# A written order for the second and third unit of an HGRN2 attention with a quick-GELU MLP, and w_in stored by pairs of blocks

## The chip, the cores and the metric

The kernel runs on one core of a Trainium2 chip. A core has TensorE (PE, matrix products; loads of its stationary operand are shown as PEld), VectorE (DVE), ScalarE (ACT), GpSimd (POOL) and SyncE (SP). SP, and here and there ACT, issue the transfers (SPq and ACTq in the profile), which the core's 16 DMA engines carry out. The metric is the device time of one execution in microseconds (us); less is better.

## The reference

Four batches, eight heads, 768 tokens and heads of 48 go through a gated linear recurrence; its output, laid out as 3072 tokens of 384, goes through an MLP with a hidden width of 2048.

```python
f = 1.0 / (1.0 + np.exp(-f_logit))
for t in range(S):
    state = f[:, :, t, :, None] * state + np.einsum('bhd,bhe->bhde', k[:, :, t], v[:, :, t])
    y[:, :, t] = np.einsum('bhd,bhde->bhe', q[:, :, t], state)
x = y.transpose(0, 2, 1, 3).reshape(B * S, H * D)
h = x @ w_in                                   # 384 -> 2048
g = h * (1.0 / (1.0 + np.exp(-1.702 * h)))
out = g @ w_out                                # 2048 -> 384
```

The weights come in as 64-bit floats; the kernel makes 32-bit floats of them itself.

## The kernel before

**Units.** The tokens go in 12 units of 256 (`U`), three to a batch. `attention(n)` makes the parts of unit n's attention, `mlp_unit` and `mlp_block` its MLP. In unit n the tokens are cut into chunks of 64. Within a chunk the recurrence goes through six levels (`level`, or `levels` two at a time from unit 2 on): PE makes scores (L442, into the tile `sc`), DVE multiplies the gates into q and k (`promote`, L536 or L540), ACT copies keys and queries aside for the next level (`set_aside`: Kc L511, Qc L517), and `evacuate` moves the scores into A (DVE L483 and L502, ACT L492). Then k is turned by PE (`turn_k`, L615, copied by ACT L616), PE adds the chunk's own products (`add`, L552) and makes the state products (L663), and DVE sums the states (L688, L689). The read-out (L710) takes the states; ACT copies it to yT (L725, `half(0)` and `half(1)`), and `to_x` sends it by transfers into xT, the MLP's operand. A half has three transfers: one of 144 KB (L777) and two of 32 and 16 KB (L782).

**Ahead of a unit's levels** its f, q and k are turned: from unit 2 on by DVE (`turn`, L361). f goes through the sigmoid on ACT (L391) and POOL (L388), and POOL makes the gates' products (`begin_gates`, L433). `load_raw` loads f (0), q (1) and k (2) of the next unit, `load_v` its v.

**Weights.** `pairs` lists 16 pairs of blocks of 128 hidden units in the order of use: for each of four rows r two pairs of w_in, then two of w_out. `fetch_weights` issues the transfer of the next pair's 64-bit words on SP's queue (768 KB; there are three buffers, `bits`, so pair m + 3 waits for the passes of pair m that read its buffer). `begin_pair` puts one ACT pass over the high words (L239) into ACT's queue at once and three DVE passes into `todo`: `low` (L235), `high` (L228, which needs ACT's pass) and `both` (L238, which writes the weights). A call of `convert` issues one of these passes, begins the next pair when few are left, and after a pair's last one calls `fetch_weights`.

**MLP of units 0 and 1.** Row by row: `mlp_h` has an item for each block (three products of 256 columns, L1125, then the gelu on ACT, L1129), `mlp_o` one for each block and half of the tokens (a product of 384 columns, L1139); ACT and DVE sum them (L1189, L1191). A row of a unit is 4 `h` items and 8 `o` items. These items are the list `fill`; each names how many blocks of weights (`state["done"]`) it needs. An `o` item needs its whole row. Unit 2 is like them at first, then uses sums of weights: `sums_of_w` makes sums of thirds of a row of blocks (`WA`, L954 and L952), and `sums_in_place` writes some of them over w_in itself, four on POOL and five on DVE. From unit 3 on the first layer is 20 products of such sums (`mlp_h20`, L1031), the second seven (`mlp_o7`, L893).

**Order.** `opening()` writes out unit 0's attention and unit 1's beginning. Then `follow(1, ...)`, `follow(2, ...)` and `follow(3, ...)` run the parts of a unit, which `parts_of` lists; behind each part `PLAN` says how many items of `fill`, conversions and chores (sums of weights) are issued. An item whose weights are not done in the program's order is left out there and comes later. To `follow(2)` the order of every engine is the one in which the program issues; later, that of PE and POOL alone. From unit 4 on `merge` spreads the items over the parts. `HOLES` puts conversions inside unit 2's levels. `keep_up` issues products that nobody reads (L116, 320 columns; each call takes one of four banks in turn), three ahead of unit 1's level 1 and three behind it.

The parts of unit 1 are: read-out of unit 0 and level 0; levels 1 to 5; two turns of k (T); states (S); its own read-out (W); turning f of unit 2 (B); turning q and loading v (B); gates and turning k with its first copies (B). Of unit 2: levels 0 and 1, 2 and 3, 4 and 5 (V); f and q of unit 3 (B); two T; k of unit 3 (B); S.

Of the kernel before, what the change touches and what calls it, by code (L numbers as in the profile page):

```python
# [23 lines left out]
def kernel(  # L24
# [33 lines left out]
    nc = tc.nc  # L58
# [108 lines left out]

    w_in = const.tile([P, NK, DFF], F32, name="w_in")
    w_out = const.tile([P, NFF, DM], F32, name="w_out")
# [25 lines left out]
    def fetch_weights(engine=nc.sync):  # L195
        n = state["fetch"]
        if n >= len(pairs) or n - PAIRS_AHEAD >= state["done"] // 2:
            return
        state["fetch"] += 1
        dst, parts = pairs[n]  # L200
        if moe_w_in.dtype == F32:
            for part, src in parts:
                nc.sync.dma_start(out=part(dst), in_=src)
            return
        bits = wp.tile([P, 2 * DM * 2], I32, tag="bits", name=f"bits_{n}", bufs=PAIRS_AHEAD)
        by_dst = bits.rearrange("p (c f) -> p c f", c=dst.shape[1])
        for part, src in parts:
            engine.dma_start(out=part(by_dst), in_=src.bitcast(I32))
        fetched[n] = by_dst.rearrange("p c (f two) -> p c f two", two=2)

    def begin_pair(m):
        if m not in fetched:
            todo.append(None)
            return
# [29 lines left out]
        todo.extend((high, both, None))  # L244

    def convert():

        if state["begin"] < len(pairs) and len(todo) <= NOP // 2:
            begin_pair(state["begin"])
            state["begin"] += 1  # L250
        if todo and todo[0]:
            todo.pop(0)()
        if todo and todo[0] is None:
            todo.pop(0)
            state["done"] += 2
            fetch_weights()


    HOLES = {(N_FILL, 0): 3, (N_FILL, 1): 2, (N_FILL, 2): 1, (N_FILL, 4): 1}

    def convert_in(n, l):

        for _ in range(HOLES.get((n, l), 0)):
            convert()

# [69 lines left out]
    def attention(n):  # L335
# [357 lines left out]
        def _():  # L693
# [26 lines left out]
            def half(h):  # L720
                for g in range(h, NG):
                    for f in (1, 0):
                        at, step = (g * HS, 1) if f else (U - 1 - g * HS, -1)
                        to, of = (rows(h), columns(h, g)) if g else (slice(0, HS + D),) * 2
                        nc.scalar.copy(view(yT[to], at, [[U, NP], [step, HS]]), py[of, g, :, f, :])  # L725
                two = (nc.scalar, nc.sync) if h and n < N_FILL else (nc.sync,)
                to_x(lambda h: (yT[rows(h), :NK], lambda r, d: yT[r:r + d, NK]), xT[:, :, :U], NG, (h,), two)
# [13 lines left out]
            xTs[n] = xT  # L741
            if n == 0:
                fetch_weights()
            if n > N_FILL:
# [181 lines left out]
    lanes = {}  # L926
    WA = {f"a{i}{c}": w_in[:, c, ROW[i] * FG * P:(ROW[i] + 1) * FG * P] for i in range(ROWS) for c in range(NK)}
    assert ROWS == 4 and NK == 3 and FG == 4

    def sums_of_w(names):  # L930

        for name in names:
            if name == "p16":
                WA[name] = wp.tile([P, 2 * DM], F32, tag="s", name="N_p16", bufs=1)[:, :FG * P]
            else:
                WA[name] = const.tile([P, FG * P], F32, name=f"N_{name}")
        first = (
            ("c3", "a30", "", "a32"), ("p15", "a21", "+", "a31"), ("c2", "a11", "+", "a12"), ("p6", "c2", "+", "a22"),
# [59 lines left out]
    def mlp_h20(n, g, before):  # L998
# [24 lines left out]
        def product(x, group, lane):  # L1023
# [5 lines left out]
            for t in range(wide):  # L1029
                f = group * wide + t  # L1030
                nc.tensor.matmul(  # L1031
                    ph[:, t], lhsT=WA[a][:, f * P:(f + 1) * P], rhs=E[n][b], start=(root and t == 0), stop=not goes_on,
                    skip_group_check=True,
# [77 lines left out]
    def mlp_h(n, ffs, g):  # L1111
        t = {}

        def one(ff, c):
            if c == 0:
# [9 lines left out]
            nc.tensor.matmul(  # L1125
                ph, lhsT=w_in[:, c, ff * P:(ff + 1) * P], rhs=xTs[n][:, c, :], start=(c == 0), stop=(c == NK - 1)
            )
# [4 lines left out]
    def mlp_o(n, ffs, g, done):  # L1132
# [3 lines left out]
        def one(tt, ff):  # L1136
# [68 lines left out]
    def parts_of(n):  # L1205
# [12 lines left out]
        if n + 1 < NALL:  # L1218
# [9 lines left out]
            else:  # L1228
# [23 lines left out]
    def merge(n, fill, columns, share):  # L1252
# [17 lines left out]
        state["behind"] = max(0, columns - done)  # L1270

    def follow(n, fill, plan):

        parts = parts_of(n)
        assert len(parts) == len(plan), (n, [kind for kind, _ in parts])
        done = 0
        for (kind, fn), (n_fill, n_ops, n_chores) in zip(parts, plan):
# [4 lines left out]
            done += 1  # L1282
            jobs = [convert] * n_ops + chores[:n_chores]
            del chores[:n_chores]
            if (n, done) == (1, 2):
                keep_up(3)
            for i in range(n_fill):
                for job in jobs[len(jobs) * i // n_fill:len(jobs) * (i + 1) // n_fill]:
                    job()
                if fill and fill[0][2] <= state["done"]:  # L1290
                    fill.pop(0)[1]()
            if not n_fill:
                for job in jobs:
                    job()

# [8 lines left out]
    def opening():  # L1304
# [44 lines left out]
        for _ in range(NOP):  # L1349
            convert()  # L1350

    fill = []
    opening()
    WAITS = {(1, "W", 1): 3}
    PLAN = {
# [4 lines left out]
    }  # L1360
# [4 lines left out]
    follow(2, fill, PLAN[2])  # L1365
    fill_order.close()
    while chores:
        chores.pop(0)()
# [47 lines left out]
```

## Time and profile before

| | |
|---|---|
| median of 3 runs | 594.89 us (593.5 to 596.12) |
| the profiled execution | 595.5 us, its span 593.2 us |
| PE busy | 568.8 us (96%) |
| weight loads on PE | 518.0 us (87%) |
| DVE busy | 438.1 us (74%) |
| ACT busy | 288.4 us (49%) |
| POOL busy | 139.2 us (23%) |
| moved by DMA | 60.34 MB, 102 GB/s in the mean |

The span is that of the instructions in one profiled execution; times in rows are microseconds from its start. In a timeline a row merges neighbouring instructions of one kind: start, duration, engine, line, operation, what is written from what, the number of records, and in brackets the idle time of the engine before and what ended it. In a table of stretches each row gives the length, then the busy time of PE, PEld, DVE, ACT and POOL with the number of instructions, the granted clock of PE (1.00 is full), the busy share of the DMA engines and GB/s. A 32-bit product appears as two records.

### The profile page before, as it was taken

The numbers are of one execution on the slowest core, as the hardware profiler recorded it, in microseconds if no ns is written. First come the engines' busy times: TensorE is split into PE (matmuls) and PEld (weight loads), VectorE is DVE, ScalarE is ACT, GpSimd is POOL, SyncE is SP. The second block draws the span as 40 slices with busy tenths as digits, with TensorE's granted clock in tenths as the row PEclk, the third lists the DMA queues.
The fourth block names the chain that finished last, engine by engine and source line by source line (L and its number), as shares of the span: only waits on it lengthen the run. The fifth ranks groups of instructions, "written<-read, shape, count | busy, mean of one in ns | idle before, by whom it ended". The sixth has DMA issues, their size and how long they took to land.

```text
span 593.2 us, 18507 instructions
## 1 busy us (share of the span) xinstructions
PE 568.8 (96%) x7832; PEld 518.0 (87%) x7832; DVE 438.1 (74%) x697; ACT 288.4 (49%) x588; POOL 139.2 (23%) x226
## 2 busy tenths in 40 slices
PE   7979888999999999999999999999999999999997
PEld 6756565867789999999999999999999999999997
DVE  2897767885989788798777798786987786461284
ACT  4754435424452474474474573573663563552440
POOL 3020020155235510600700700700701602203000
PEclk9989988999999999999999999999999999999999
DMA  7869958352363353453452343453352121001000
GB/s 185 189 183 221 232 138 223 75 129 61 104 150 75 104 124 82 98 127 90 121 140 57 86 114 94 118 143 63 92 146 59 46 55 29 28 3 27 28 1 28
DMA packets 86771, 60.34 MB, mean 102 GB/s; under 512 B 33505, under 2 KB 78465, under 8 KB 86689
## 3 DMA queue, kind: packets, MB, share of 16 engines
q1 hardware_dynamic: 86128, 58.40, 39.7%
q8 instruction: 62, 1.02, 0.7%
q10 hardware_dynamic: 561, 0.75, 0.5%
q14 instruction: 20, 0.16, 0.1%
HBM read 45.49 MB, written 8.91 MB: 92 GB/s over the span
## 4 chain that ended last, share of the span: by engine, by line
PE 83%; DVE 6%; ACT 5%; DMA 3%; issue 2%; ACTq 1%; SPq 0%; DVEq 0%
PE h L1031 16%; PE o_Y L893 13%; PE h L1125 10%; PE o_Z L893 9%; PE sc L442 6%; PE h_y L1031 6%; PE o L1139 6%; PE o_X L893 5%; PE o_W L893 4%; DMA bits<-in_moe_w_in_dram 2%; PE y L710 2%; PE y L552 2%; PE sc L663 2%; DVE X L540 1%; DVE g L1059 1%
## 5 line engine op out<-in xcount | busy, mean ns | idle before, releaser
L540 DVE TENSOR_TENSOR X<-X,tot 128x1024 f32<-128x1024 f32 x50 | 67.6, 1351 | 39.7 <-PE sc L442 31.4
L511 ACT COPY Kc<-X 128x512 f32<-128x512 f32 x72 | 48.2, 669 | 80.2 <-DVE X L540 62.9
L1125 PE MATMUL h<-xT,w_in 128*128 128x256 f32 x288 | 66.9, 389 | 3.1 <-DMA xT<-yT 1.5
L993 POOL TENSOR_TENSOR E<-xT 128x128 f32<-128x128 f32 (+1 forms) x36 | 16.0, 453 | 227.3 <-DMA xT<-yT 227.3
L1125 PEld LDWEIGHTS h<-xT,w_in 128*128 128x128 f32 x288 | 55.3, 194 | 13.1 <-DMA xT<-yT 2.1
L1031 PE MATMUL h<-E,w_in 128*128 128x128 f32 (+1 forms) x476 | 62.8, 277 | 0.5 <-DVE g L1059 0.5
L1031 PEld LDWEIGHTS h<-E,w_in 128*128 128x128 f32 x476 | 57.4, 192 | 1.4 <-issue 0.9
L893 PE MATMUL o_Y<-T,S 128*128 128x192 f32 x320 | 57.6, 329 | 0.0
L1061 ACT ACTIVATE g<-g 128x512 f32<-128x512 f32 (+1 forms) x70 | 40.3, 589 | 26.9 <-DVE g L1059 26.8
L893 PEld LDWEIGHTS o_Y<-T,S 128*128 128x128 f32 x320 | 52.3, 190 | 0.5
L1059 DVE TENSOR_TENSOR g<-g,h 128x512 f32<-128x512 f32 (+1 forms) x58 | 36.2, 638 | 15.4 <-PE h L1031 14.4
L1139 PE MATMUL o<-w_out,g 128*128 128x384 f32 x128 | 45.9, 508 | 0.7 <-ACT g L1129 0.7
L361 DVE STREAM_TRANSPOSE X<-raw 128x512 f32<-128x512 f32 x40 | 42.3, 1117 | 3.1 <-PE y L710 2.7
L502 DVE COPY_PREDICATED A<-masks,sc 128x256 f32<-128x256 uint32 (+1 forms) x98 | 41.9, 504 | 0.0
L1139 PEld LDWEIGHTS o<-w_out,g 128*128 128x128 f32 x128 | 24.4, 197 | 16.3 <-issue 1.5
L725 ACT COPY yT<-y 48x256 f32<-48x256 f32 (+1 forms) x66 | 21.1, 369 | 29.2 <-PE y L710 28.8
L442 PE MATMUL sc<-X,Kc 48*64 48x64 f32 x1344 | 28.6, 222 | 6.5 <-ACT Kc L511 4.9
L442 PEld LDWEIGHTS sc<-X,Kc 48*64 48x64 f32 x1344 | 24.4, 136 | 10.7 <-ACT Kc L511 6.8
L1050 ACT ACTIVATE g<-h 128x512 f32<-128x512 f32 (+1 forms) x52 | 28.4, 576 | 8.6 <-PE h L1031 8.3
L388 POOL TENSOR_SCALAR F<-F 128x1024 f32<-128x1024 f32 x10 | 12.9, 1286 | 81.0 <-ACT F L391 81.0
L1129 ACT ACTIVATE g<-h 128x256 f32<-128x256 f32 x48 | 17.7, 382 | 26.1 <-PE h L1125 25.7
L893 PE MATMUL o_X<-w_out,g 128*128 128x192 f32 x160 | 29.9, 332 | 0.5 <-ACT o_X L857 0.5
(161 smaller groups left out, 1193.5 us busy)
## 6 DMA issues: line engine op xcount, KB each, us to landing
bits<-in_moe_w_out_dram SPq DMA_DIRECT2D x8, 768.0 KB
raw<-in_f_logit_dram SPq DMA_DIRECT2D x48, 96.0 KB, 2.3
raw<-in_k_dram SPq DMA_DIRECT2D x48, 96.0 KB, 2.6
bits<-in_moe_w_in_dram SPq DMA_DIRECT2D x8, 576.0 KB
raw<-in_q_dram SPq DMA_DIRECT2D x44, 96.0 KB, 2.4
k_tok<-z SPq DMA_DIRECT2D x64, 64.0 KB, 1.6
kt<-k_tok SPq DMA_DIRECT2D x16, 256.0 KB
out_dram<-osb SPq DMA_DIRECT2D x20, 192.0 KB, 1.9
```

The source lines that it names most:

```text
L361: nc.vector.transpose(view(out, at, [[HALF, NP], [step, R4], [R4 * step, 32]]), by_half[:, j, f].rearrange("p a (j d) -> p (a j) d", j=R4) ...
L442: nc.tensor.matmul(t["sc"][h][g * HS:(g + 1) * HS, a, s, :], lhsT=t["Kc", l][rows(h), x:x + HS], rhs=rhs(h, a, g), start=True, stop=True,)
L502: moved = nc.vector.copy_predicated(out=view(A, c * HALF + at, dims), mask=mask.bitcast(U32), data=got)
L511: nc.scalar.copy(c.rearrange("p (n two m) -> p n two m", two=2, m=m), view(X, KF * SLOT, [[2 * m, SLOT // (2 * m)], [(KR - KF) * SLOT + m, ...
L540: nc.vector.tensor_tensor(x, x, y, ALU.mult)
L893: nc.tensor.matmul(t[name], lhsT=lhs(f), rhs=rhs(f), start=(new and i == 0), stop=(i == HF - 1), skip_group_check=True,)
L1031: nc.tensor.matmul(ph[:, t], lhsT=WA[a][:, f * P:(f + 1) * P], rhs=E[n][b], start=(root and t == 0), stop=not goes_on, skip_group_check=True,)
L1050: nc.scalar.activation(to, ph, AF.Copy, scale=float(sign))
L1059: nc.vector.tensor_tensor(to, to, part, ALU.add if sign > 0 else ALU.subtract)
L1061: nc.scalar.activation(to, to, AF.Gelu_apprx_sigmoid)
L1125: nc.tensor.matmul(ph, lhsT=w_in[:, c, ff * P:(ff + 1) * P], rhs=xTs[n][:, c, :], start=(c == 0), stop=(c == NK - 1))
L1139: nc.tensor.matmul(t["po"], lhsT=g[ff // FG][:, ff % FG, tt * P:(tt + 1) * P], rhs=w_out[:, ff, :], start=(ff == ffs[0]), stop=(ff == ffs[ ...
```

## The change

- `w_in` is stored by pairs: [128, 8 pairs, 3, 256] for [128, 3, 2048], so a pair is one run of 768 values in a partition for three runs of 256. Products address it accordingly; an entry of `WA` is two runs of 256.
- `follow` reads strings. A letter is a step: f an item of `fill`, c a conversion, p the beginning of the next pair (ACT's pass), w a fetch, s a chore, k one keep-up product. `convert` no longer fetches. An item or a fetch that is not ready in the program's order is an error.
- An `o` item needs only the pair of w_out that holds its block.
- Plan of unit 1: 21 conversions for 27, nine keep-up products for six, 28 items for 32 issued; the eight items and four conversions between its read-out and the turn of unit 2's f are gone, but for the beginning of a pair and a fetch. Its loads of q and k of unit 2 come one part later. `HOLES` has nine conversions for seven, unit 2's plan 15 for 11, and 56 items for 51. Unit 3's plan is the same list in letters.
- In unit 1's `half(1)` the transfers go SP, ACT, SP for ACT, SP, ACT.

```diff
-    w_in = const.tile([P, NK, DFF], F32, name="w_in")
+    w_in = const.tile([P, NFF // 2, NK, 2 * P], F32, name="w_in")
...
-            pairs.append((w_in[:, :, f], [
+            pairs.append((w_in[:, ff // 2], [
...
-        if n >= len(pairs) or n - PAIRS_AHEAD >= state["done"] // 2:
-            return
+        assert n < len(pairs) and n - PAIRS_AHEAD < state["done"] // 2
...
-    def convert():
-
-        if state["begin"] < len(pairs) and len(todo) <= NOP // 2:
+    def begin_next():
+
+        if state["begin"] < len(pairs):
             begin_pair(state["begin"])
             state["begin"] += 1
+
+    def convert():
+
+        if len(todo) <= NOP // 2:
+            begin_next()
         if todo and todo[0]:
             todo.pop(0)()
         if todo and todo[0] is None:
             todo.pop(0)
             state["done"] += 2
-            fetch_weights()
-
-
-    HOLES = {(N_FILL, 0): 3, (N_FILL, 1): 2, (N_FILL, 2): 1, (N_FILL, 4): 1}
+
+
+    HOLES = {(N_FILL, 0): "ccp", (N_FILL, 1): "cwcc", (N_FILL, 2): "cwp", (N_FILL, 3): "cc", (N_FILL, 4): "cw"}
...
-                two = (nc.scalar, nc.sync) if h and n < N_FILL else (nc.sync,)
+                two = ((nc.scalar, nc.sync), (nc.sync, nc.scalar))[n] if h and n < N_FILL else (nc.sync,)
...
-    WA = {f"a{i}{c}": w_in[:, c, ROW[i] * FG * P:(ROW[i] + 1) * FG * P] for i in range(ROWS) for c in range(NK)}
+    WA = {f"a{i}{c}": w_in[:, ROW[i] * FG // 2:(ROW[i] + 1) * FG // 2, c, :] for i in range(ROWS) for c in range(NK)}
...
-                ph, lhsT=w_in[:, c, ff * P:(ff + 1) * P], rhs=xTs[n][:, c, :], start=(c == 0), stop=(c == NK - 1)
+                ph, lhsT=w_in[:, ff // 2, c, ff % 2 * P:(ff % 2 + 1) * P], rhs=xTs[n][:, c, :], start=(c == 0), stop=(c == NK - 1)
...
-        return [(DM, lambda tt=tt, ff=ff: one(tt, ff), (ff // FG + 1) * NPC) for tt in range(U // P) for ff in ffs]
+        return [(DM, lambda tt=tt, ff=ff: one(tt, ff), ff // FG * NPC + FG + 2 + ff % FG // 2 * 2) for tt in range(U // P) for ff in ffs]
...
-                    for i, j in ((1, 0), (3, 1), (4, 2)):
+                    for i, j in ((1, 0), (4, 1), (5, 2)):
                         followed(i, lambda j=j: load_raw(n + 1, j))
...
+    def follow_steps(steps):
+
+        for step in steps:
+            if step == "f":
+                assert fill[0][2] <= state["done"], (fill[0], state)
+                fill.pop(0)[1]()
+            elif step == "c":
+                convert()
+            elif step == "p":
+                begin_next()
+            elif step == "w":
+                fetch_weights()
+            elif step == "s":
+                for job in chores[:1]:
+                    chores.remove(job)
+                    job()
+            else:
+                keep_up(1)
+
     def follow(n, fill, plan):
...
-            keep_up(WAITS.get((n, kind, done), 0))
             fn()
...
+            follow_steps(steps)
...
-    WAITS = {(1, "W", 1): 3}
+    FIRST = 'k'
     PLAN = {
...
-        1: ((0, 6, 2), (1, 1, 13), (2, 3, 0), (8, 4, 6), (3, 2, 0), (0, 0, 0), (0, 2, 0), (1, 2, 0), (1, 3, 0), (8, 4, 0),
-            (3, 0, 1), (3, 0, 0), (2, 0, 0)),
-        2: ((8, 2, 0), (6, 3, 1), (14, 6, 0), (0, 0, 3), (5, 0, 10), (11, 0, 0), (0, 0, 6), (7, 0, 3)),
+        1: (
+            "cccwcccwkkkkk", "kkkcf", "cfccwf", "fcffcwffcffcf", "ffcc", "f", "cwc", "fcc", "ffcf", "pw", "fw", "ff",
+            "fffffff",
+        ),
+        2: (
+            "ffff", "ffffffff", "fcfcfcwffcfcfcwfffcfcfcff", "sss", "fcfcfcfffffss", "fcfcfcffffffff", "",
+            "fffffffffff",
+        ),
     }
...
+    follow_steps(FIRST)
     follow(1, fill, PLAN[1])
```

More of the change, by code (lines that the diff above doesn't have):

```diff
@@ L255, in convert @@
             state["done"] += 2
-            fetch_weights()
-    HOLES = {(N_FILL, 0): 3, (N_FILL, 1): 2, (N_FILL, 2): 1, (N_FILL, 4): 1}
+    HOLES = {(N_FILL, 0): "ccp", (N_FILL, 1): "cwcc", (N_FILL, 2): "cwp", (N_FILL, 3): "cc", (N_FILL, 4): "cw"}
     def convert_in(n, l):
-        for _ in range(HOLES.get((n, l), 0)):
-            convert()
+        follow_steps(HOLES.get((n, l), ""))
     def load_raw(n, j, engines=(nc.sync,)):
@@ L741, in _ @@
             xTs[n] = xT
-            if n == 0:
-                fetch_weights()
             if n > N_FILL:
@@ L1031, in product @@
                 nc.tensor.matmul(
-                    ph[:, t], lhsT=WA[a][:, f * P:(f + 1) * P], rhs=E[n][b], start=(root and t == 0), stop=not goes_on,
+                    ph[:, t], lhsT=WA[a][:, f // 2, f % 2 * P:(f % 2 + 1) * P], rhs=E[n][b], start=(root and t == 0), stop=not goes_on,
                     skip_group_check=True,
@@ L1275, in follow @@
         assert len(parts) == len(plan), (n, [kind for kind, _ in parts])
-        done = 0
-        for (kind, fn), (n_fill, n_ops, n_chores) in zip(parts, plan):
+        for (kind, fn), steps in zip(parts, plan):
             if kind in ("S", "S1"):
                 assert not any(in_y.get(m) for m in range(n))
-            keep_up(WAITS.get((n, kind, done), 0))
             fn()
[L1282 to L1294, printed above, removed]
+            follow_steps(steps)
     chores = []
@@ L1350, in opening @@
             convert()
+        fetch_weights()
     fill = []
     opening()
-    WAITS = {(1, "W", 1): 3}
+    FIRST = 'k'
     PLAN = {
[4 rows of a table removed]
+        3: (
+            "fffffffsffsf", "fsffsffsf", "f", "fsfsfsffsfsfsf", "", "ffff", "ff", "ffffffffffffffffsffsf", "fffsf",
+        ),
[6 more added lines that the diff above has]
+            "fffffffffff",
+        ),
     }
@@ L1365 @@
     follow(2, fill, PLAN[2])
+    assert state["fetch"] == len(pairs)
     fill_order.close()
+    assert state["done"] == 2 * len(pairs) or moe_w_in.dtype == F32
     while chores:
```

2 lines of the change are left out of this document (added), and 1 row of the table PLAN.

## The prediction

> **What bounds the kernel now.** I read the page first, then who TensorE (PE) waited for, then 2 us stretches, then the timelines of 28 to 125 us.
>
> ```profile
> span 593.2 us, 18507 instructions
> ...
> GB/s 185 189 183 221 232 138 223 75 129 61 104 150 75 104 124 82 98 127 90 121 140 57 86 114 94 118 143 63 92 146 59 46 55 29 28 3 27 28 1 28
> ...
> PE 83%; DVE 6%; ACT 5%; DMA 3%; issue 2%; ACTq 1%; SPq 0%; DVEq 0%
> ```
>
> The chain that ended last is PE work for 83%. The waits of PE's instructions in 28 to 125 us (us in total, times, longest):
>
> ```profile
> PE sc L442 <- ACT Kc L511: 4.9, 2, 2.8
> PE sc L442 <- DVE A L502: 1.6, 1, 1.6
> PE h L1125 <- DMA xT<-yT: 1.5, 1, 1.5
> PE h L1125 <- DVE w_in L238: 1.3, 2, 1.1
> PE y L710 <- ACT y L674: 1.3, 1, 1.3
> PE o L1139 <- ACT g L1129: 0.7, 1, 0.7
> PE h L1125 <- issue: 0.3, 1, 0.3
> ```
>
> They sum to 11.6 us. The stretches below (PE, weight load, DVE, ACT, POOL busy, then granted clock) show what comes on top, and what follows later:
>
> ```profile
> 74.00:76.00 2.00, 1.79 (x5) 1.30 (x5) 2.00 (x4) 0.00 (x0) 0.00 (x0) 0.67 0.88 324
> 76.00:78.00 2.00, 2.00 (x6) 1.54 (x5) 2.00 (x3) 1.15 (x2) 0.00 (x0) 0.50 1.06 310
> ...
> 98.00:100.00 2.00, 2.00 (x38) 1.33 (x30) 1.41 (x3) 0.06 (x1) 0.00 (x0) 0.64 0.78 116
> 100.00:102.00 2.00, 2.00 (x4) 1.09 (x4) 1.55 (x2) 1.08 (x2) 0.00 (x0) 0.51 0.98 379
> ...
> 86.00:136.00 50.00, 45.65 (x468) 32.90 (x467) 39.63 (x55) 19.03 (x38) 9.73 (x6) 0.97 0.57 139
> ...
> 118.00:560.00 442.00, 438.27 (x6256) 413.60 (x6255) 330.74 (x501) 220.57 (x439) 123.01 (x188) 1.00 0.35 87
> ```
>
> Two us times one minus the clock is 1.7 us lost at 74 to 78 and 1.7 at 98 to 102; with 1.2 at 38 (below) that is 4.6. Behind 118 us PE is busy for 438.3 of 442 us. So this stage bounds: all products are fixed work, and a microsecond that PE gains ahead of 118 us arrives at the end whole. The most that can be had is 16 us.
>
> **The change part by part.** PE's timeline (start, us; a first-layer item, L1125, is six records, a second-layer item, L1139, or a keep-up product two):
>
> ```profile
> 33.05 1.88 PE L116 MATMUL idle<-masks,ident 128*128 128x320 f32 x6
> 37.04 1.11 PE L442 MATMUL sc<-X,Kc 48*64 48x64 f32 x32 [2.10 <-ACT Kc L511]
> 38.08 3.08 PE L116 MATMUL idle<-masks,ident 128*128 128x320 f32 x6
> 55.47 2.43 PE L1125 MATMUL h<-xT,w_in 128*128 128x256 f32 x10 [1.07 <-DVE w_in L238]
> 64.56 1.11 PE L710 MATMUL y<-X,st 48*48 48x64 f32 x64
> 73.51 0.70 PE L1125 MATMUL h<-xT,w_in 128*128 128x256 f32 x2 [1.49 <-DMA xT<-yT]
> 74.42 11.88 PE L1125 MATMUL h<-xT,w_in 128*128 128x256 f32 x46 [0.21 <-DVE w_in L238]
> 86.23 0.70 PE L442 MATMUL sc<-Qc,Kc 48*64 48x64 f32 x32
> 90.34 5.43 PE L1139 MATMUL o<-w_out,g 128*128 128x384 f32 x16
> 106.67 10.52 PE L1125 MATMUL h<-xT,w_in 128*128 128x256 f32 x48
> ```
>
> Hence an `h` item is 10.52/8 = 1.31 us, an `o` item 5.43/8 = 0.68, a keep-up 1.88/3 = 0.63.
>
> *Keep-ups, nine for six.* One goes in front of unit 0's read-out, into the 1.3 us wait for L674. Five in place of three stand ahead of the level-1 score: 3.1 us inside a gap of 4 us (33.05 to 37.04), so free; without that cover the three more would cost 1.9. The other three ran at half clock (3.08 against 1.88). If the fuller gap keeps the clock, 1.2 is gained, if not, 0; I take 0.5, below the middle, because `xT` must have landed too.
>
> [...]
>
> *w_in by pairs.* The two rows with `w_in L238` as releaser wait for a conversion that they don't read: at 55.47 the product is of block 1's first pair and the conversion is of its second; at 74.42 the product is of block 0 and the conversion of block 2. In the old layout a pair is three strips, and their hull covers the neighbours. Contiguous pairs end it: 1.1 + 0.2 = 1.3 us. The write itself stays: L238 has 768 elements either way.
>
> *Conversions and fetches later.* Six passes of DVE (two pairs) move from ahead of unit 2's transposes to behind them:
>
> ```profile
> L235 DVE TENSOR_SCALAR a<-bits 128x768 int32<-128x768 uint32 x16 | 10.1, 628 | 1.1 <-DMA bits<-in_moe_w_in_dram 1.1
> L228 DVE TENSOR_SCALAR s<-bits 128x768 int32<-128x768 int32 x16 | 9.3, 582 | 12.9 <-ACT bits L239 12.9
> L238 DVE CUSTOM_DVE_ANT_0 w_out<-s,a 128x1536 uint16<-128x1536 uint16 x8 | 7.7, 957 | 0.2
> L540 DVE TENSOR_TENSOR X<-X,tot 128x1024 f32<-128x1024 f32 x5 | 6.1, 1225 | 1.5 <-ACT Qc L517 0.9 <-PE sc L442 0.6
> ...
> 67.28 0.92 ACT L239 ACTIVATE bits<-bits 128x768 f32<-128x768 f32 x1 [4.99 <-DMA bits<-in_moe_w_in_dram]
> 68.36 1.96 ACT L725 COPY yT<-y 112x256 f32<-112x256 f32 x6
> 84.03 0.83 ACT L511 COPY Kc<-X 128x512 f32<-128x512 f32 x1
> ...
> 74.75 2.02 DVE L361 STREAM_TRANSPOSE F<-raw 128x512 f32<-128x512 f32 x2
> ```
>
> A pair is 0.63 + 0.58 + 0.96 = 2.2 us of DVE, two are 4.3; they return beside unit 2's levels. There (86 to 136 us) DVE had 39.6 us of work; with these 4.3 it has 43.9, beside PE's 45.6 and the four `h` items of block 1 that now come behind the first score (5.2), 50.8 together: covered. If that cover were gone, 4.3 us would be the price. Pair 8's L239 stands in ACT's queue, waits 4.99 us for its bits, and the last gelu of block 1 and unit 1's copies (68.36) queue behind it. The new order has L239 behind the copies. The gelu's 0.7 us of PE goes. The copies start when the read-out ends, about 65.9 (64.56, less 1.1, plus two `o` items of 0.68 now ahead of it, plus 1.1 for itself): 2.5 us earlier. `xT` landed 73.51 - 68.36 = 5.2 us behind the start of the copies. Half 1 now issues two of its three transfers on SP and one on ACT, so SP's fifth issue (about 0.6) is late: `xT` is there at 71.7. PE comes to it at 65.9 + 6 x 0.68 = 70.0, so a wait of 1.6 stays (the 1.5 is not gained), and with it perhaps its half clock (1.7): gone or not, I take 0.85.
>
> *f turned right behind states.* The transposes of f, q, k (six at about a microsecond) start about 65.6 for 74.75, k is done by 72 for some 81, and the Kc copy is no longer behind six first-layer items' gelus: 72 for 84.03. PE reaches the level-0 score at 71.7 + 4 x 1.31 = 76.9 (before 86.23, with four items more). By then level 0 is multiplied in (72 + 1.4 for two copies + 1.2) and Kc of level 1 copied (75.5): the 2.8 us wait goes. PE then does the four `h` items of block 1, to 83.3; `sc` is free after L540 (78.0 to 79.2), two copies (1.3), L540 again and A's passes (2.0): 83.7. A wait of 0.5 stays of 1.6: 1.0 gained (0 to 1.6). The next score comes behind eight `o` items at 90.3, DVE frees `sc` about 90.1: nothing. With these waits gone, so is the half clock of 98 to 102: 1.7 (0 if the small waits suffice to bring it).
>
> *Sums in place.* Each third of a block (`WA`) is now two runs, whose hulls overlap. DVE's five sums into w_in must follow POOL's in the same block. Their first reader on PE comes behind 200 us: nothing, but see the second rival. One transfer moved from ACT to SP, chores moved on POOL: nothing: POOL has 9.7 us of work in those 50.
>
> *Sum:* 0.5 + 1.3 + 0.7 + 0.85 + 2.8 + 1.0 + 1.7 = 8.85 us. The profiled execution took 595.5 us with a span of 593.2; its successor is then a span of 584.4 and 586.6 us. The median of the runs stands 0.6 below the profiled one: **586.0 us**. With every upper bound (0.7, 0.85, 0.6, and the 1.6 at `xT`) it is 582.3; with the lower ones (0.5 + 0.85 + 1.0 + 1.7 gone) 590.1.
>
> **Rivals.** *Landing decides.* In 44 to 74 us (slices 4 and 5) the DMA engines move 221 and 232 GB/s, about the most of the span, and
>
> ```profile
> bits<-in_moe_w_in_dram SPq DMA_DIRECT2D x8, 192.0 KB, 6.3
> ...
> 60.51 2.49 SPq L208 DMA_DIRECT2D bits<-in_moe_w_in_dram x4
> ```
>
> a pair lands 6.3 us behind its issue. Pair 9 went out in the row at 60.51; now it is queued behind unit 1's `xT` transfers, about 70. It lands at 76.3; its L239 (0.9) stands ahead of level 1's Kc copy (0.6), which PE wants at 77.5: 0.3 late, as good as nothing. If it lands a pair later (0.79 MB at 230 GB/s, 3.4 us), PE waits 3.7 and the half clock returns (1.7): 591.4. For it: ACT's wait of 4.99 us. Against: fewer fetches stand in the queue by then.
>
> *DVE behind POOL (the slower side).*
>
> ```profile
> 165.98 1.49 DVE L954 TENSOR_TENSOR w_in<-w_in,N_c 128x512 f32<-128x512 f32 x1 [0.38 <-PE h L1125]
> 168.60 1.09 DVE L623 STREAM_TRANSPOSE z<-X 128x512 f32<-128x512 f32 x1
> ...
> 176.82 3.20 POOL L954 TENSOR_TENSOR w_in<-w_in 128x512 f32<-128x512 f32 x2 [9.89 <-PE h L1125]
> 178.26 1.15 PE L663 MATMUL sc<-vt,kn 64*64 64x48 f32 x64
> ```
>
> DVE's first sum in place runs at 165.98, POOL's first two at 176.82 to 180.0. If it keeps its place in DVE's order, it now waits 14 us for POOL, and the transpose of k at 168.60 behind it feeds the product at 178.26: PE waits nearly 14, 600 us. It decides from 12 us on. Against: DVE's sums have waits of 0.4 us here, so the order follows what they wait for, and it may follow the new one.
>
> *The layout does nothing* (the waits have another cause): 1.3 less, 587.3.
>
> **How the numbers follow.** The forecast 0.62; layout without effect 0.07; landing decides 0.20, half of it on either side of 591.9; DVE behind POOL 0.11, of which 0.08 end over 597.9. A measurement of this kernel can tell 0.5%, 3 us. Faster is 0.62 + 0.07 + 0.10 = 0.79, same 0.10 + 0.03 = 0.13, slower 0.08. The range, 582 to 592, holds the bounds and most of the landing case.
>
> **What would show it.** Right: no wait of L1125 for `w_in L238`; L361's F ahead of 70 us; the level-0 score of unit 2 about 77 us without a wait for Kc behind it; the granted clock whole at 98 to 102. Wrong: ACT waiting for bits ahead of a Kc copy, a `sc` wait on A of over a microsecond, new waits of PE behind 118 us, above all a DVE wait for POOL L954 at 160 to 185.

## The result, and the profile after

| | before | after |
|---|---|---|
| median, us | 594.51 (593.5 to 596.12) | 587.29 (586.66 to 587.77) |
| span of the profiled execution, us | 593.2 | 585.4 |
| waits of PE, 28 to 125 us | 11.6 | 5.7 |
| half clock in 28 to 125 us, us lost | 5.1 | 0 |

The ratio is 0.9875, 95% interval 0.9851 to 0.99: 7.2 us less, where 8.9 were forecast. The 5.1 us are three periods of 3.41 us at half clock, at 37.12, 74.67 and 98.56; the prediction counted 1.2 of the first one's 1.7. The line numbers move by two or three: L1127 is the first-layer item, L1141 the second-layer item, L445 the score, L514 and L520 Kc and Qc, L364 the turns, L543 the gates' products, L1193 DVE's sum of the second layer, L956 and L954 the sums of weights.

Two lines of the page, and the waits of PE's instructions in 28 to 125 us (us in total, times, longest):

```profile
span 585.4 us, 18532 instructions
...
PE 73%; DVE 10%; DMA 7%; SPq 4%; ACT 3%; issue 2%; ACTq 0%; DVEq 0%
```

```profile
PE sc L445 <- ACT Kc L514: 2.1, 2, 1.2
PE h L1127 <- DMA xT<-yT: 1.8, 1, 1.8
PE y L555 <- ACT A L495: 1.0, 1, 1.0
PE sc L445 <- DVE A L505: 0.6, 1, 0.6
PE y L713 <- ACT y L677: 0.2, 1, 0.2
```

The row for `w_in L238` is gone, the Kc wait fell from 4.9 to 2.1, the A wait from 1.6 to 0.6. Of the stretches that showed half clock before (length, then PE, PEld, DVE, ACT and POOL busy, granted clock) two are shown; all four read 1.00:

```profile
76.00:78.00 2.00, 1.26 (x35) 1.14 (x36) 0.95 (x2) 1.75 (x6) 0.69 (x2) 1.00 1.36 240
...
98.00:100.00 2.00, 2.00 (x11) 1.71 (x9) 1.97 (x4) 1.09 (x3) 0.00 (x0) 1.00 0.43 101
```

PE's timeline, with the places of unit 2 that the prediction put a time to (the scores of its levels 0, 2 and 4 are the rows that read `Qc` at 74.83, 83.41 and 89.92):

```profile
62.24 1.11 PE L713 MATMUL y<-X,st 48*48 48x64 f32 x64
63.47 4.11 PE L1141 MATMUL o<-w_out,g 128*128 128x384 f32 x12
69.36 5.55 PE L1127 MATMUL h<-xT,w_in 128*128 128x256 f32 x24 [1.78 <-DMA xT<-yT]
74.83 0.69 PE L445 MATMUL sc<-Qc,Kc 48*64 48x64 f32 x32
76.74 0.70 PE L445 MATMUL sc<-X,Kc 48*64 48x64 f32 x32 [1.21 <-ACT Kc L514]
...
83.41 0.69 PE L445 MATMUL sc<-Qc,Kc 48*64 48x64 f32 x32 [0.59 <-DVE A L505]
89.92 0.69 PE L445 MATMUL sc<-Qc,Kc 48*64 48x64 f32 x32
...
127.58 4.15 PE L1127 MATMUL h<-xT,w_in 128*128 128x256 f32 x18 [0.82 <-ACT g L1131]
```

The second-layer items run on behind the read-out, there is one wait for `xT` of 1.78 us, and the level-0 score comes at 74.83 in place of 86.23 (where four first-layer items more stood ahead of it). The level-4 score of the kernel before:

```profile
104.19 0.70 PE L442 MATMUL sc<-Qc,Kc 48*64 48x64 f32 x32
```

It had done six second-layer items (4.1 us) more by then. So at this score PE stands 104.19 - 89.92 - 4.1 = 10.2 us ahead of the kernel before. Of these 10.2, 7.8 arrive at the end. The first piece given back is the row at 127.58, a wait that the kernel before did not have. Then come 0.25 for `kn` at 169.49 and 1.1 more on the gelu's products that DVE makes in later units: the row for `h_y` among the waits behind 118 us, which read 1.4, 2, 0.7 before:

```profile
PE h_y L1033 <- DVE g L1061: 2.5, 3, 0.9
...
PE h L1127 <- ACT g L1131: 0.8, 1, 0.8
```

DVE's and POOL's timelines show where the wait at 127.58 comes from:

```profile
108.30 1.63 DVE L235 TENSOR_SCALAR a<-bits 128x768 int32<-128x768 uint32 x1
109.86 1.62 DVE L228 TENSOR_SCALAR s<-bits 128x768 int32<-128x768 int32 x1
111.51 1.91 DVE L238 CUSTOM_DVE_ANT_0 w_out<-s,a 128x1536 uint16<-128x1536 uint16 x1
...
121.71 2.04 DVE L364 STREAM_TRANSPOSE X<-raw 128x512 f32<-128x512 f32 x2
...
158.00 1.03 DVE L956 TENSOR_TENSOR w_in<-w_in,N_c 128x512 f32<-128x512 f32 x1
```

```profile
107.54 1.98 POOL L956 TENSOR_TENSOR N_c<-w_in 128x512 f32<-128x512 f32 x1
109.48 1.58 POOL L956 TENSOR_TENSOR N_p<-w_in 128x512 f32<-128x512 f32 x1
```

The same two sums in the kernel before:

```profile
106.54 2.20 POOL L954 TENSOR_TENSOR N_c<-w_in 128x512 f32<-128x512 f32 x1 [24.03 <-DVE w_in L238]
...
125.09 2.04 POOL L954 TENSOR_TENSOR N_p<-w_in 128x512 f32<-128x512 f32 x1
```

The three passes of a pair, 0.63, 0.58 and 0.96 us in the mean of the kernel before, take 1.63, 1.62 and 1.91 while POOL adds weights. Before, all but one of POOL's first five sums ran behind 125 us; now all run from 107.5 to 116, beside the passes that the new plan moved. Then ACT's timeline:

```profile
123.78 0.85 ACT L514 COPY Kc<-X 128x512 f32<-128x512 f32 x1 [3.97 <-DVE X L364]
...
126.56 0.68 ACT L514 COPY Kc<-X 128x512 f32<-128x512 f32 x1 [1.35 <-DVE X L543]
127.15 1.20 ACT L1131 ACTIVATE g<-h 128x256 f32<-128x256 f32 x4
```

Unit 3's k is turned at 121.71. ACT's first copy of it waits for that until 123.78, its next copy for DVE's product behind the turn; four gelus stand behind both copies, and PE waits for one of these.

### The profile page after: what moved, and what is told of

The parts are those of the page before. It is cut to its first block, busy times and chain, and to the rows that moved or that the text cites. A ratio compares the mean times of both kernels' runs of the same rounds, so it can differ in the third digit from the quotient of the medians.

```text
span 585.4 us, 18532 instructions
## 1 busy us (share of the span) xinstructions
PE 564.4 (96%) x7838; PEld 514.6 (88%) x7838; DVE 441.0 (75%) x697; ACT 288.8 (49%) x588; POOL 142.5 (24%) x226
## 4 chain that ended last, share of the span: by engine, by line
PE 73%; DVE 10%; DMA 7%; SPq 4%; ACT 3%; issue 2%; ACTq 0%; DVEq 0%
PE h L1033 17%; PE o_Y L894 14%; PE o_Z L894 9%; PE h_y L1033 6%; PE sc L445 6%; PE o_X L894 5%; PE o_W L894 4%; DMA bits<-in_moe_w_in_dram 3%; PE h L1127 3%; PE o L1141 3%; DVE X L364 2%; PE y L713 2%; PE y L555 2%; PE sc L666 2%; DVE X L543 1%
## 5 line engine op out<-in xcount | busy, mean ns | idle before, releaser
L543 DVE TENSOR_TENSOR X<-X,tot 128x1024 f32<-128x1024 f32 x50 | 67.7, 1354 | 44.7 <-PE sc L445 38.4
L514 ACT COPY Kc<-X 128x512 f32<-128x512 f32 x72 | 48.4, 672 | 81.6 <-DVE X L543 61.2
L1127 PE MATMUL h<-xT,w_in 128*128 128x256 f32 x288 | 65.9, 383 | 2.6 <-DMA xT<-yT 1.8
L1127 PEld LDWEIGHTS h<-xT,w_in 128*128 128x128 f32 x288 | 53.7, 190 | 12.3 <-issue 2.4
L364 DVE STREAM_TRANSPOSE X<-raw 128x512 f32<-128x512 f32 x40 | 42.4, 1115 | 3.1 <-PE y L713 1.8
L1141 PE MATMUL o<-w_out,g 128*128 128x384 f32 x128 | 43.7, 491 | 0.1
L1141 PEld LDWEIGHTS o<-w_out,g 128*128 128x128 f32 x128 | 23.7, 190 | 14.9 <-ACT g L1131 0.4
L728 ACT COPY yT<-y 48x256 f32<-48x256 f32 (+1 forms) x66 | 21.1, 370 | 29.3 <-PE y L713 28.9
L445 PE MATMUL sc<-X,Kc 48*64 48x64 f32 x1344 | 28.3, 220 | 3.7 <-ACT Kc L514 2.1
L445 PEld LDWEIGHTS sc<-X,Kc 48*64 48x64 f32 x1344 | 24.1, 134 | 8.0 <-ACT Kc L514 4.4
L894 PE MATMUL o_W<-T,g 128*128 128x192 f32 x160 | 29.5, 331 | 0.0
```

The lines of the kernel that those rows point to most:

```text
L364: nc.vector.transpose(view(out, at, [[HALF, NP], [step, R4], [R4 * step, 32]]), by_half[:, j, f].rearrange("p a (j d) -> p (a j) d", j=R4) ...
L445: nc.tensor.matmul(t["sc"][h][g * HS:(g + 1) * HS, a, s, :], lhsT=t["Kc", l][rows(h), x:x + HS], rhs=rhs(h, a, g), start=True, stop=True,)
L514: nc.scalar.copy(c.rearrange("p (n two m) -> p n two m", two=2, m=m), view(X, KF * SLOT, [[2 * m, SLOT // (2 * m)], [(KR - KF) * SLOT + m, ...
L543: nc.vector.tensor_tensor(x, x, y, ALU.mult)
L894: nc.tensor.matmul(t[name], lhsT=lhs(f), rhs=rhs(f), start=(new and i == 0), stop=(i == HF - 1), skip_group_check=True,)
L1127: nc.tensor.matmul(ph, lhsT=w_in[:, ff // 2, c, ff % 2 * P:(ff % 2 + 1) * P], rhs=xTs[n][:, c, :], start=(c == 0), stop=(c == NK - 1))
```

## The experiments

Each kernel was measured beside the kernel before on the same chip, and a ratio is to that one; differences from the changed kernel (587.29) are between chips. The kernel before had a median of 595.52 us beside the old layout, the layout alone and the two changes of pairs 8 and 9; 594.32 beside the six keep-up products, the order of the queues and the shortened sums; 594.15 beside the later sums, all three edits and the changed kernel again; 595.34 beside the two kernels with keep-up products that come last.

### The two halves of the change

**Old layout, new plan.** The changed kernel with four lines undone:

```diff
-    w_in = const.tile([P, NFF // 2, NK, 2 * P], F32, name="w_in")
+    w_in = const.tile([P, NK, DFF], F32, name="w_in")
...
-            pairs.append((w_in[:, ff // 2], [
+            pairs.append((w_in[:, :, f], [
...
```

> The changed kernel with w_in stored as before (three strips for each pair), all else as changed. Theory (a strip's hull makes products wait for conversions of other pairs): the first item of unit 1's block 1, at 77.4 us, must wait for pair 9's last pass (79.7), and the first item of block 2, at 96.3, for that of pair 12 (99.6); the wait shows on the second of an item's three products. About 5 us slower than the changed kernel (3 to 8), 592. Rival (the two waits seen before had another cause, and the layout does nothing): no such waits, 587.3, within 0.5.

594.36 us (593.61 to 597.57), ratio 0.9988 (0.9969 to 1.0007): 7.1 slower than the changed kernel, within the theory's 3 to 8. The whole gain is gone. PE's waits and timeline:

```profile
PE h L1127 <- DVE w_in L238: 5.1, 3, 2.8
```

```profile
77.58 0.70 PE L1127 MATMUL h<-xT,w_in 128*128 128x256 f32 x2
79.97 6.70 PE L1127 MATMUL h<-xT,w_in 128*128 128x256 f32 x22 [1.69 <-DVE w_in L238]
```

The first product of the item at 77.58 runs, its second waits for the conversion of a pair that it doesn't read. The item of block 2 waits 2.81 at 102.89 in the same way. Half clock follows at 80.3 and 104.2, 1.7 us each: 5.1 us of waits and 3.4 of half clock that the changed kernel does not have.

**New layout, old plan.** The kernel before with the layout alone.

> The kernel before with w_in stored by pairs and nothing else. Theory: the waits for w_in L238 at 55.5 (1.07 us) and 74.4 (0.21) go: 1.3 us faster than before (0.5 to 2), 593.2. Rival (what PE saves there, it waits elsewhere, since ACT holds the copies until pair 8 has landed): no gain, 594.5.

594.5 us (593.36 to 599.51), ratio 0.9998 (0.9978 to 1.0018). No gain shows, as the rival said, but the interval ends where the theory's 1.3 us would lie (0.9978). The waits:

```profile
PE sc L442 <- ACT Kc L511: 5.2, 2, 2.8
PE h L1126 <- DMA xT<-yT: 1.7, 1, 1.7
PE sc L442 <- DVE A L502: 1.3, 1, 1.3
```

No row for `w_in L238` is left, as the prediction said. The rival's reason, that PE waits elsewhere for what it saves, is not what the trace shows: the level-0 score comes at 84.70 for 86.23 and the level-1 score at 88.21 for 89.71, with about the same Kc wait between (2.81 for 2.78). Half clock took 5.1 us in both. The span is 591.5 us for 593.2, but this execution (593.5) is among the fastest of its twelve. So whether the layout alone is worth nothing or some 1 us stays open; neither half alone gains as much as 2 us by its interval, and together they gain 7.

### The steps ahead of 80 us

**Six keep-up products for nine.** Without the one ahead of the read-out, two of five ahead of the level-1 score:

```diff
-    FIRST = 'k'
+    FIRST = ''
...
-            "cccwcccwkkkkk", "kkkcf", "cfccwf", "fcffcwffcffcf", "ffcc", "f", "cwc", "fcc", "ffcf", "pw", "fw", "ff",
+            "cccwcccwkkk", "kkkcf", "cfccwf", "fcffcwffcffcf", "ffcc", "f", "cwc", "fcc", "ffcf", "pw", "fw", "ff",
```

> The changed kernel with six keep-up products for nine: none ahead of unit 0's read-out, three ahead of level 1. Theory (the fuller gap keeps the clock): the granted clock falls to about half at 37 to 41 us again, the three keep-ups behind level 1 take 3.1 us for 1.9: 1.2 us slower, 588.5 (588 to 589). Rival (the clock there does not depend on them): 587.3, the clock at 1.00.

587.05 us (586.64 to 589.23), ratio 0.9869 (0.9837 to 0.9902), as the rival said. In the profiled execution the clock was whole from 28 to 125 us with six as well, and the three at 36.68 took 1.88 us. The three more are worth nothing that can be measured. That the clock never depends on them is not shown: the mean clocks of the six executions were 0.993 to 1.000, those of ten executions of the changed kernel 0.997 to 1.000, and only one of the six was profiled.

**Order of the queues as before.**

```diff
-                two = ((nc.scalar, nc.sync), (nc.sync, nc.scalar))[n] if h and n < N_FILL else (nc.sync,)
+                two = (nc.scalar, nc.sync) if h and n < N_FILL else (nc.sync,)
```

> The changed kernel with unit 1's second half sent as before: two of its three transfers issued by ACT, one by SP. Step of the prediction (SP's fifth issue delays xT): PE's wait for xT falls from 1.8 to about 1.2, 0.6 us faster, 586.7, as ACT's pass for pair 8 waits for its bits anyway. Rival (the last transfer waits for an earlier landing, whoever issues it; or ACT is held up): 587.3 or up to 0.6 slower.

588.26 us (586.49 to 592.07), ratio 0.9891 (0.9854 to 0.9928): not the 0.6 us faster of the prediction's step, and not told apart from the changed kernel. PE waits for `xT` in two pieces, and not for less:

```profile
70.86 0.67 PE L1127 MATMUL h<-xT,w_in 128*128 128x256 f32 x2 [1.28 <-DMA xT<-yT]
72.63 6.67 PE L1127 MATMUL h<-xT,w_in 128*128 128x256 f32 x22 [1.10 <-DMA xT<-yT]
```

That is 2.4 us for 1.78, and in this execution half clock follows at 73.6 (1.7 us lost).

**Pair 9's ACT pass not begun ahead of the level-1 copy.**

```diff
-    HOLES = {(N_FILL, 0): "ccp", (N_FILL, 1): "cwcc", (N_FILL, 2): "cwp", (N_FILL, 3): "cc", (N_FILL, 4): "cw"}
+    HOLES = {(N_FILL, 0): "cc", (N_FILL, 1): "cwcc", (N_FILL, 2): "cwp", (N_FILL, 3): "cc", (N_FILL, 4): "cw"}
```

> The changed kernel without the early beginning of pair 9 ahead of level 0's multiplication (its ACT pass then stands behind level 1's Kc copy). Theory (ACT waits 4.2 us for pair 9's bits with level 1's Kc copy behind it, and that is PE's wait of 1.2 us at the level-1 score): that wait goes, 0.6 to 1.2 us faster, 586.4. Rival (DVE's high pass needs the ACT pass and stands ahead of level 1's multiplication, so the wait only moves to the next score): 587.3, with the wait for A at the level-2 score grown from 0.6 to 1.8.

586.6 us (586.17 to 588.35), ratio 0.9859 (0.9835 to 0.9883). PE's timeline:

```profile
76.29 0.65 PE L445 MATMUL sc<-X,Kc 48*64 48x64 f32 x32
...
83.42 0.69 PE L445 MATMUL sc<-Qc,Kc 48*64 48x64 f32 x32 [1.09 <-DVE A L505]
```

The 1.21 us wait at 76.74 is gone, and the one for A at 83.4 is 0.5 longer. What that is worth can't be read from single profiles: here level 2 comes 20.25 us behind the read-out (63.17), in the changed kernel's profile 21.17, and in a second profile of the changed kernel (below) 20.16, with a wait for Kc of only 0.19. The times can't tell the two kernels apart either. Whether pair 9's bits hold the copy up by 1.2 or by 0.2 differs from run to run.

**Pair 8's passes ahead of the turn of f.**

```diff
-            ... "ffcf", "pw", "fw", "ff",
+            ... "ffcf", "pwccc", "fw", "ff",
...
-    HOLES = {(N_FILL, 0): "ccp", (N_FILL, 1): "cwcc", ...
+    HOLES = {(N_FILL, 0): "p", (N_FILL, 1): "wcc", ...
```

> The changed kernel with the three DVE passes of pair 8 back ahead of the turn of unit 2's f (behind unit 1's read-out), so the turn is no longer right behind the states. Theory (the early turn is what takes away PE's waits at unit 2's first scores): pair 8 lands at 67.7, so f is turned about 70 for 63.2, the Kc copy comes at 76 for 69.5, PE waits some 2.8 us at the level-0 and level-1 scores beyond today's 1.2, perhaps with half clock behind it: 590 to 592. Rival (the landing of pair 9 decides the level-1 copy anyway, so the turn has time to spare): 587.3 to 588.

593.9 us (591.83 to 595.15), ratio 0.9966 (0.9946 to 0.9987): worse than either theory said, and through a wait that neither had. DVE and PE:

```profile
69.12 0.56 DVE L235 TENSOR_SCALAR a<-bits 128x768 int32<-128x768 uint32 x1 [3.72 <-DMA bits<-in_moe_w_in_dram]
```

```profile
75.91 1.56 PE L1127 MATMUL h<-xT,w_in 128*128 128x256 f32 x6 [1.69 <-DVE sum L1193]
81.08 1.75 PE L1127 MATMUL h<-xT,w_in 128*128 128x256 f32 x6 [3.61 <-DVE sum L1193]
```

DVE waits for pair 8's bits, the turns and the sums of the second layer (L1193) stand behind, and PE's items wait for the PSUM banks that these sums have yet to empty: 5.3 us. Half clock at 82.3 to 89.2 comes on top (3.4 us lost). Nearly the whole gain is lost, 6.6 of 7.2 us. So turning f right behind the states matters by what no longer stands ahead of it in DVE's queue.

### The wait behind 118 us

**POOL's first five sums cut to 16 columns of 512.** The other columns stay zero, so this kernel leaves out a part of the later first layers. In `sum_of_w`, for the first five:

```diff
+        if out in early and few:
+            few.pop()
+            engine.tensor_tensor(*(WA[i][:, :, :8] for i in (out, x, y)), ALU.add if op else ALU.subtract)
+            return
```

> The changed kernel with the first five sums of weights on POOL (ahead of unit 3) cut to 16 of 512 columns, the rest left at zero, so a part of unit 3's and later first layers is left out. Theory (POOL's sums at 107 to 116 us make DVE's passes beside them two to three times as long, DVE turns unit 3's k late, ACT's Kc copy holds gelus, and PE waits 0.8 us at 127.6): DVE's passes of pairs 14 and 15 take 0.56, 0.56 and 0.95 us for 1.6, 1.6 and 1.9, and the wait at 127.6 goes: 0.8 us faster, 586.5. Rival (DVE's other work there, the T sums, makes it late): the passes are short, the wait stays, 587.3.

586.09 us (584.8 to 586.78), ratio 0.9845 (0.981 to 0.988), 1.2 less than the changed kernel; the intervals of the two ratios overlap. DVE's timeline (lines are four higher here):

```profile
108.96 0.56 DVE L239 TENSOR_SCALAR a<-bits 128x768 int32<-128x768 uint32 x1 [0.32 <-DMA bits<-in_moe_w_out_dram]
109.98 0.56 DVE L232 TENSOR_SCALAR s<-bits 128x768 int32<-128x768 int32 x1 [0.46 <-ACT bits L243]
110.57 0.96 DVE L242 CUSTOM_DVE_ANT_0 w_out<-s,a 128x1536 uint16<-128x1536 uint16 x1
```

The passes are back to their durations, and the wait at 127.58 is gone. From the level-4 score to the end the trace takes 493.6 us, the two of the changed kernel 495.5 and 494.7. The next kernel moves the whole sums, and there too the passes are short and the wait is gone: the collision with POOL's sums was its cause.

**The five sums whole, but later.** The computation is whole here:

```diff
-            "ffff", "ffffffff", "fcfcfcwffcfcfcwfffcfcfcff", "sss", "fcfcfcfffffss", "fcfcfcffffffff", "",
+            "ffff", "ffffffff", "fcfcfcwffcfcfcwfffcfcfcff", "", "fcfcfcfffff", "fcfcfcffffffff", "",
```

> The changed kernel with the first five two-input sums of POOL (107.5 to 116 us there) handed out behind unit 2's plan instead of inside it; the computation is whole. Theory (POOL's sums double DVE's passes of pairs 14 and 15, which makes k of unit 3 late and costs the 0.8 us wait for a gelu at 127.6): those passes take 0.56, 0.56 and 0.96 us again, the wait at 127.6 goes, and the time is 586.2 to 586.5 us, as with the shortened sums (586.1). Rival (the collision only moves): the five sums now run beside DVE's work of unit 3's states behind 118 us, those DVE operations grow instead, PE waits there for as long, and the time stays at 587.3.

591.93 us (588.95 to 593.7), ratio 0.9949 (0.993 to 0.9969). The passes took 0.55, 0.56 and 0.96 us and the wait at 127.58 went, as the theory said, but the time is 4.6 us worse, and not by the slower operations that the rival expected. DVE's waits in 118 to 180 us, and PE:

```profile
DVE N_p L954 <- POOL N_c L956: 10.6, 1, 10.6
```

```profile
143.24 0.69 PE L445 MATMUL sc<-Qc,Kc 48*64 48x64 f32 x32 [1.87 <-DVE A L505]
144.90 1.14 PE L445 MATMUL sc<-X,Kc 48*64 48x64 f32 x32 [0.97 <-ACT Kc L514]
```

One sum is DVE's (L954, into N_p) and needs one of POOL's. In the changed kernel it waits 4.2 us for it, in a gap of DVE's work; now 10.6, with the level's products (L543) and A's passes behind it. PE waits 2.8 us, and half clock comes for two periods from 144.48 on (3.4 us lost). The sums can't simply go later, because a DVE instruction in a fixed place reads them. This is the prediction's second rival (DVE behind POOL) at another sum, brought about by hand.

### Trying for a better kernel

**All three edits.** The last one, pair 9's pass, and two keep-up products in the wait for `xT`:

```diff
-            "fffffff",
+            "fffkkffff",
```

> c1_sums_later, and pair 9's pass of ACT not begun ahead of level 1's copy, and two keep-up products inside the wait for unit 1's xT; the computation is whole. Theory (three separate waits): the wait for level 1's Kc is gone, the wait at 127.6 too, and the two keep-ups (1.3 us) lie inside the wait of 1.8 us and cost nothing: 585.5 to 586.0 us. Rival (the waits ahead of 90 us are one chain and only change their name): as c1_sums_later, and if xT lands up to 0.7 us earlier than in the trace, the keep-ups cost that much: 586.2 to 587.0.

596.76 us (592.63 to 598.1), ratio 1.0018 (0.9991 to 1.0045): some 10 us above both the theory and the rival. **The changed kernel again**, on the same chip:

> The changed kernel itself once more, beside the other two on one chip. Both theories: 587.3 us; its spread (0.4 to 0.6) says what can be told between the three.

587.38 us (586.23 to 589.23), ratio 0.9877 (0.9851 to 0.9904), as at first. In its profile the read-out came at 64.56, 2.3 us later than in the first one, level 2 at 84.72, 1.3 later, and the span was 585.9, 0.5 longer: the head of the program differed by 2.3 us between the two. Here it had half clock between 14.6 and 29.3 us (8 tenths granted in that slice) and a wait of 0.87 for unit 0's `xT` at 40.90, which the first profile did not have. Behind the read-out the waits were shorter: the one for Kc by 1.0, the row for `h_y` by 1.1 (it was 1.4 again).

Beside the loss of the later sums, the combined kernel showed a wait of 2.67 us at 73.44 for DVE's sum L1193. Two more kernels look for its cause.

**Two keep-up products alone.**

> The changed kernel with two keep-up products between unit 0's last second-layer item and the first first-layer item of unit 1, nothing else; the computation is whole. Theory (each keep-up takes the next of four banks in turn, so the second first-layer item behind them meets the bank that DVE's sum of the second layer, L1193, frees only at about 73): that item waits 2 to 3 us for L1193, half clock may follow it, the level-0 score stands at 78 to 81 us for 74.8, and the time is 590 to 593 us. Rival (the wait came from moving POOL's sums or from pair 9's pass, which c2_all_three changed as well): no wait for L1193, 587.3 us.

591.31 us (589.86 to 593.46), ratio 0.9921 (0.9886 to 0.9956): the theory, with no half clock behind the wait. PE's timeline:

```profile
68.77 1.24 PE L116 MATMUL idle<-masks,ident 128*128 128x320 f32 x4
70.73 1.53 PE L1127 MATMUL h<-xT,w_in 128*128 128x256 f32 x6 [0.72 <-DMA xT<-yT]
74.74 4.15 PE L1127 MATMUL h<-xT,w_in 128*128 128x256 f32 x18 [2.47 <-DVE sum L1193]
```

**Four keep-up products** at the same place ("fffkkkkffff").

> As e1_two_keepups with four keep-up products at the same place; the computation is whole. Theory (the turn of the four banks): each item meets the same bank as in the changed kernel, no wait for L1193; four take 2.5 us in a wait of 1.8, so up to 0.7 later: 587.3 to 588.2 us. Rival (keep-ups there hold PE up for DVE's sum whatever their number, or cost what they take): as e1_two_keepups or slower, 590 us and more.

593.76 us (592.6 to 594.65), ratio 0.9964 (0.9937 to 0.9991). The theory, no wait and at most 588.2, was wrong; the time is that of the rival.

```profile
73.70 1.44 PE L116 MATMUL idle<-masks,ident 128*128 128x320 f32 x2 [4.18 <-DVE sum L1193]
```

Half clock comes for two periods here, from 72.69 to 79.52 (3.4 us lost). The cause, a bank, is the same, and the miss came from counting only first-layer items. By the order in which the four banks are taken, it is the fourth taker behind the second-layer items that meets the bank that L1193 empties: the second item behind two keep-ups, and the fourth keep-up itself. With none it is the fourth item, which in the changed kernel finds the bank empty (L1193 ends at 72.93, the item starts about 73.3) and in the kernel with six keep-ups waited 0.42 for it. A keep-up product whose result nobody reads still takes a bank.

No version beats the changed kernel by more than the measurement can tell; 586.6 without pair 9's early pass is the lowest with the whole computation.

## Why the prediction was right

The time came out at 587.3 for 586.0 (range 582 to 592), and most steps held. For the sum's 8.85 the spans differ by 7.8 and the medians by 7.2. The term that failed is the one called covered; the keep-ups' clock and the first half clock were sized too small, and the Kc wait too large. That the total is so near is in part luck: the gain up to the level-4 score came to 10.2, more than the sum had, and 2.4 were given back behind it, where the sum had nothing.

- **"a microsecond that PE gains ahead of 118 us arrives at the end whole": too strong.** Of 10.2 us at the level-4 score 7.8 arrived, and of the 2.3 by which the two profiles of the changed kernel differ at the read-out, 0.5 did. PE is busy for nearly all of what follows, but its waits there differ: `h_y` reads 0.6 with the old layout, 1.4 in the kernel before and in the second profile of the changed kernel, 2.5 in its first and without pair 9's early pass. It does not simply follow how early PE comes: all three edits together, with a span of 594.8, have 2.4. What sets it stays open.
- **Where the steps stood:** predicted level-0 score 76.9, level 2 at 83.8, level 4 at 90.3; measured 74.83, 83.41, 89.92. The turn of f began at 63.23 for 65.6. The read-out came 2.6 us ahead of its place: the half clock at 37 us (the level-2 score came 5.3 us behind the level-1 score, now 3.7), a level-1 score 0.4 earlier and the issue (0.3) make up most of it, which the steps had not counted there.
- **Keep-ups, 0.5 of 0 to 1.2:** the clock stayed whole, so the term came out above its bound in this trace, at the 1.6 just named: the score ran at half clock before as well. But the nine are not shown to be the reason: with six it was whole too. There PE waited 1.48 us at the level-1 score, the kernel before 2.10; what shortened that wait stays open. The step "the fuller gap keeps the clock" is not borne out.
- **w_in by pairs, 1.3:** the mechanism was right, and the size depends on the plan. Under the old plan the layout is worth at most the 1.3 us, and no gain could be measured; under the new one it is worth 7 us, because the new plan puts conversions beside items of other pairs. The sum counted the false waits that the trace of before had, and not those that the new plan would have brought.
- **Level-1 wait for Kc, 2.8:** it went but for 1.21 in one profile and 0.19 in the other, and what stayed is the mechanism of the first rival, pair 9's L239 waiting for its bits ahead of the copy (ACT's timeline):

```profile
75.17 0.94 ACT L239 ACTIVATE bits<-bits 128x768 f32<-128x768 f32 x1 [4.21 <-DMA bits<-in_moe_w_in_dram]
76.01 0.68 ACT L514 COPY Kc<-X 128x512 f32<-128x512 f32 x1
```

  The bits were there at 75.2 for 76.3, but PE wanted the copy at 75.5 for 77.5.
- **A wait, 1.0 of 1.6, and `xT`'s 1.6 stays:** 0.59 and 1.78 were left; right. That SP's fifth issue costs 0.6 did not show: with the old order of queues `xT` is waited for 2.4 us in all.
- **Half clock at 74 to 78 and 98 to 102:** both gone; the first was counted half (0.85 for 1.7). The half clock at 37 us stood in the sum only as a part of the keep-ups' term.
- **"Conversions later: covered", and chores "nothing": wrong.** DVE's 4.3 us were weighed against PE's work with the durations of before. Beside POOL's sums the passes take two to three times as long (1.63, 1.62 and 1.91 us for 0.63, 0.58 and 0.96), DVE is busy for 15.97 of the 16 us from 102 to 118, and a wait of 0.82 comes at 127.58. With POOL's sums shortened the wait goes, and the median is 1.2 us lower. The prediction had weighed POOL's 9.7 us against 50 of room, and not what they do to DVE.
- **Rivals:** landing decided a wait of 1.2, not the outcome. DVE behind POOL at the sums in place did not come: DVE's is at 158.00, POOL's two follow from 167.60. The layout did not do nothing.

## What to carry to other kernels

A layout that makes a block's write contiguous is worth what the schedule around it lets collide (here no gain that could be measured under the old order, 7.1 us under the new one): price it under the new order, not by the waits in the old trace. Of work moved into another engine's stretch, ask what the two do to each other's durations (a pass of 0.56 us took 1.63), and which in-order instruction downstream reads its result (DVE waited 10.6 us for a sum moved later). A filler product is not free because PE waits there: it takes a buffer in turn, and the buffer's owner may be the next thing waited for (2.47 us behind two of them here).

## What the runs showed of the hardware

**Half clock came behind stretches in which PE was partly idle.** The granted clock fell to 0.50 for 3.41 us (the kernel before) or for 6.83 (the later sums, 144.48 to 151.31), and within a run the starts lie a whole number of 3.41 us apart: before at 37.12, 74.67 and 98.56 (11 and 7 periods between), old layout with new plan at 80.30 and 104.20 (7). A window is here a stretch of 3.41 us that lies a whole number of these periods from a fall of its run. The window ahead of two periods in a row, and the first of the two, in the kernel with the later sums (stretches as above):

```profile
141.07:144.48 3.41, 0.99 (x33) 0.59 (x32) 3.38 (x6) 1.39 (x3) 1.23 (x1) 1.00 0.44 94
144.48:147.89 3.41, 2.99 (x35) 2.12 (x36) 2.78 (x7) 0.83 (x2) 0.00 (x0) 0.50 0.61 169
```

In the traces with a fall between 28 and 125 us, PE was idle in the window just ahead of each for 1.57 us (before, 95.14 to 98.55) to 3.17 (four keep-ups, 69.28 to 72.69); in the stretch above for 2.42. Windows there with 1.46 or less were not followed by a fall from the full clock, and some with more were not either (1.68 at 71.18 with the layout alone, 1.86 at 75.50 with pair 8's passes first). No threshold follows from this. In the profile of before a wait of 2.8 us at 87 to 90 fell on two windows, 1.4 in each, and cost no clock; the same wait in the kernel with the layout alone fell into one (2.81, 84.84 to 88.25), and half clock came at 88.25 (1.7 us lost). The windows lie differently in each run (80.30 is 12.65 periods behind 37.12). That the same wait costs another 1.7 us or not by where it falls fits these two runs and is not shown beyond them.

**DVE and POOL beside each other.** The passes took 1.63, 1.62 and 1.91 us beside POOL's sums (128x512 out of two tiles, 1.47 to 1.98 us each), 0.56, 0.56 and 0.96 with these sums shortened. They started 1.56 and 1.65 us apart beside them, POOL's sums 1.54 to 1.94. What ties the two together is not shown.
